# Block attention and a squared-ReLU FFN in one kernel: FFN blocks of four pairs, and one list schedule for all engines

## The chip, the core and the metric

The kernel runs on one core of a Trainium2 chip. The metric is the device time of one execution in microseconds (us); lower is better. The engines are named as the profile names them: PE (TensorE, matmuls; PEld is its weight load), DVE (VectorE), ACT (ScalarE), POOL (GpSimd), SP (SyncE, which issues the DMAs).

## What is computed

```python
def reference(q, k, v, moe_w_in, moe_w_out):        # q, k, v: (8, 8, 576, 64) f32
    # attention inside chunks of 64 positions, each head apart
    scores = q_c @ k_c.T / sqrt(64);  scores -= scores.max(-1)
    attn = exp(scores);  attn /= attn.sum(-1) + 1e-9
    x = (attn @ v_c) -> (4608 tokens, 512)          # heads side by side
    # FFN
    h = x @ w_in                                    # 512 -> 2048, weights in f64
    return (maximum(h, 0) ** 2 @ w_out).astype(f32) # 2048 -> 512
```

## The kernel before

A **pair** is two chunks of 64 positions, 128 tokens of all 8 heads. There are 36 pairs. The FFN runs over **blocks** of pairs, and `blocks` (line 63) is `[4] + [3] * 10 + [2]`: one block of four pairs, ten of three, one of two. For each block and each of the 16 slices `f` of the hidden dimension there is a `Step` (line 608). `mm_in` (L623) makes the hidden slice `h`, 12 matmuls whose moving operand is as wide as the block (128 columns a pair: 512, 384 or 256). ACT and DVE then make `g` from it: `relu`, `square`, `high` (the part `gh` that PE's reduced format holds) and `low` (the rest, `gl`). `mm_out` (L667) adds `g @ w_out` into one PSUM bank a pair, `o`: three matmuls of 512 columns a pair, so 12, 9 or 6 a step. The outs of slice `f` stand two slices behind its ins (`LAG`).

Attention comes in two kinds. The first eight pairs (`NN`) are done whole, as `Pair` (line 487), during the start and block 0. The other 28 pairs are done as 56 **units** of four heads each, in a stacked form: `qst` and `kst` hold high and low parts of q and k in the two halves of the partitions, so that one 256-column matmul a head gives a product at full precision. A unit has on PE four score matmuls `sc` (L353), two transposes `pt` of the probabilities (L403) and four value matmuls `xt` (L437). Between them ACT, DVE and POOL empty the banks, make the softmax, and put `x` into `xh` and `xl`, which are the FFN's input of the *next* block. Two DMAs a unit (`pst<-pst`, L419) copy the high part of the probabilities to the other half of the partitions; the stack of a pair (lines 297 to 318) does the same with four DMAs, `qst<-ql` (L310) and `kst<-kst` (L314).

What sets the order: block 0 with all weight conversion is ordered by a small list scheduler inside the kernel (`Plan`, line 711, used by `first_block`). From block 1 on, only PE's order is written out: `merge` spreads the attention pieces evenly, one matmul at a time, between the FFN matmuls, and the order of the other engines is left to the outer scheduler, with the FFN's ACT and DVE work at a raised priority (`PRIO`). The PSUM banks of attention are two, `at0` and `at1`, taken in turn.

Of the kernel before, what the change touches and what calls it, by code (L numbers as in the profile page):

```python
# [10 lines left out]
F32 = mybir.dt.float32  # L11
# [9 lines left out]
def kernel(  # L21
# [40 lines left out]
    PRIO = 300  # L62
    blocks = [4] + [3] * 10 + [2]
    LAG = 2
    HEAD = 1
    REST = 0
# [10 lines left out]
    NN = sum(blocks[:2]) + 1  # L77
# [13 lines left out]

    early = ctx.enter_context(ExitStack())
    wst = early.enter_context(tc.tile_pool(name="wst", bufs=1))
# [16 lines left out]
    def open_late():  # L110

        early.close()
        pool = ctx.enter_context(tc.tile_pool(name="late", bufs=2))
        late["pool"] = pool
        late["q"] = pool.tile([P, H, 2, CH], F32R, name="qst", tag="qst", bufs=1)
        late["p"] = pool.tile([P, 2, HP, 2, 2, CH], F32R, name="pst", tag="pst", bufs=1)
        load_v(NN)
        nc.gpsimd.memset(late["p"].bitcast(F32), 0.0)
        late["k"] = pool.tile([P, 2, 2, H, CH], F32R, name="kst", tag="kst", bufs=1)
        for c in range(2):  # L120
            r = slice((1 - c) * CH, (2 - c) * CH)
            nc.gpsimd.memset(late["k"].bitcast(F32)[r, 1, c], 0.0)
# [120 lines left out]
    def load_qk(pair):  # L243


        pairs[pair] = {}
        for nm, src in (("q", q), ("k", k)):
            t = raw.tile([P, H, IH, 32], F32, name=f"{nm}_raw{pair}", tag=f"{nm}_raw")
            pairs[pair][nm] = t
            for c in range(2):  # L250
                bb, n0 = divmod(2 * pair + c, NCH)
                for dh in range(DH):
                    r0 = c * D + dh * 32
                    for ih in range(IH):
                        i0 = n0 * CH + ih * 32
                        s = src[bb, :, i0:i0 + 32, dh * 32:(dh + 1) * 32]
                        nc.sync.dma_start(out=t[r0:r0 + 32, :, ih, :], in_=s.rearrange("h i d -> i h d"))

    def load_v(pair):


        if pair < NN:
            for c in range(2):
                bb, n0 = divmod(2 * pair + c, NCH)
                for h2, r in enumerate(halves):
                    s = v[bb, h2:H:2, n0 * CH:(n0 + 1) * CH, :]
                    nc.sync.dma_start(
                        out=vbd[slot_of(pair)][r, :, c, h2, :], in_=s.rearrange("h i d -> i h d")
                    )
            return  # L270
        pairs[pair]["v"] = []
        for c in range(2):
            t = late["pool"].tile([P, H, D], F32, name=f"v_raw{pair}_{c}", tag="v_raw")
            pairs[pair]["v"].append(t)
            bb, n0 = divmod(2 * pair + c, NCH)
            s = v[bb, :, n0 * CH:(n0 + 1) * CH, :].rearrange("h i d -> i h d")
            for r in halves:
                nc.sync.dma_start(out=t[r], in_=s)

    def transpose_pair(pair):  # L280

        for nm in "qk":
            t = late["pool"].tile([P, H, CH], F32, name=f"{nm}t{pair}", tag=f"{nm}t", bufs=1)
            nc.vector.transpose(
                t.rearrange("p h i -> p (h i)"), pairs[pair][nm].rearrange("p h a d -> p (h a d)")
            )
            pairs[pair][nm] = t
        if pair + 1 < NPAIR:
            load_qk(pair + 1)

    def s1(u):
        b, pair, j, hq = units[u]
        if hq == 0:
            yield lambda: transpose_pair(pair)
            yield lambda: stack_qk(pair)

    def stack_qk(pair):

        qt, kt = pairs[pair]["q"], pairs[pair]["k"]
        kst = late["k"]
        qst = late["q"]
        low = late["pool"].tile([P, H, CH], F32R, name=f"ql{pair}", tag="kk", bufs=1)
        for c, (own, oth) in enumerate(other):
            nc.scalar.copy(qst[own, :, c], qt[own])  # L306
        for c, (own, oth) in enumerate(other):
            nc.vector.tensor_tensor(low[own], qt[own], qst.bitcast(F32)[own, :, c], op=ALU.subtract)
        for c, (own, oth) in enumerate(other):
            nc.sync.dma_start(out=qst.bitcast(F32)[oth, :, c], in_=low.bitcast(F32)[own])  # L310
        for c, (own, oth) in enumerate(other):
            nc.scalar.copy(kst[own, 0, c], kt[own])
        for c, (own, oth) in enumerate(other):
            nc.sync.dma_start(out=kst.bitcast(F32)[oth, 0, c], in_=kst.bitcast(F32)[own, 0, c])  # L314
        for c, (own, oth) in enumerate(other):
            nc.vector.tensor_tensor(
                kst[own, 1, c], kt[own], kst.bitcast(F32)[own, 0, c], op=ALU.subtract
            )

    def split_v(u):  # L320
        yield lambda: stack_v(u)

    def stack_v(u):


        b, pair, j, hq = units[u]
        vs = late["pool"].tile([P, 2, HP, 2, D], F32R, name=f"vs{u}", tag="vs")
        ust[u]["v"] = vs
        for c, t in enumerate(pairs[pair]["v"]):
            vr = t[:, hq * HQ:(hq + 1) * HQ].rearrange("p (a b) d -> p a b d", b=2)  # L330
            nc.scalar.copy(vs[:, c], vr)  # L331
            for h2, r in enumerate(halves):
                dst = (r, slice(None), 1 - h2)
                nc.gpsimd.tensor_tensor(  # L334
                    vs[:, c][dst], vr[dst], vs.bitcast(F32)[:, c][dst], op=ALU.subtract
                )
        if hq == NQ - 1 and pair + 1 < NPAIR:
            load_v(pair + 1)

    def s2(u):  # L340


        st = ust[u]
        b, pair, j, hq = units[u]

        def mm2(h):
            if h % 2 == 0:
                st.setdefault("sc", []).append(
                    bank(("at", next(turn_at) % 2), [P, 2, 2, 2, CH], f"sc{u}_{h}")
                )  # L350
            ps = st["sc"][-1][:, h % 2]
            hh = hq * HQ + h
            nc.tensor.matmul(  # L353
                ps.rearrange("p w c j -> p (w c j)"), late["q"][:, hh].rearrange("p c i -> p (c i)"), late["k"][:, :, :, hh],
                start=True, stop=True,
            )

        def half(h):
            if h == 0:
                st["e"] = late["pool"].tile([P, HQ, CH], F32, name=f"e{u}", tag="e", bufs=2)  # L360
            ps, e = st["sc"][h // 2], st["e"][:, h:h + 2]
            for c, r in enumerate(halves):
                nc.scalar.copy(e[r], ps[r, :, 1, c])  # L363
            for c, r in enumerate(halves):
                nc.vector.tensor_tensor(e[r], ps[r, :, 0, c], e[r], op=ALU.add)  # L365

        def rest():
            e = st["e"]
            m = att.tile([P, HQ, 1], F32, name=f"m{u}", tag="m", bufs=2)
            z = att.tile([P, HQ, 1], F32, name=f"z{u}", tag="z", bufs=2)  # L370
            nc.vector.tensor_reduce(m, e, axis=AX.X, op=ALU.max)
            nc.vector.tensor_tensor(e, e, m.broadcast_to([P, HQ, CH]), op=ALU.subtract)
            nc.scalar.activation(e, e, AF.Exp, scale=QSCALE)
            st["e"] = (e, z)

        for h in range(HQ):
            yield lambda h=h: mm2(h)
            if h % 2:
                yield lambda h=h: half(h - 1)
        yield rest  # L380

    def norm(u):
        st = ust[u]

        def f():
            e, z = st["e"]
            nc.vector.tensor_reduce(z, e, axis=AX.X, op=ALU.add)
            nc.vector.tensor_scalar_add(z, z, 1e-9)
            nc.vector.reciprocal(z, z)  # L389
            nc.gpsimd.tensor_tensor(e, e, z.broadcast_to([P, HQ, CH]), op=ALU.mult)  # L390
            st["p"] = e

        yield f

    def s3(u):

        st = ust[u]

        def tr(hp):
            if hp == 0:  # L400
                st["pt"] = bank(("at", next(turn_at) % 2), [P, HP, 2, CH], f"pt{u}")
            ps = st["pt"]
            nc.tensor.transpose(  # L403
                ps[:, hp].rearrange("p a b -> p (a b)"),
                st["p"][:, 2 * hp:2 * hp + 2].rearrange("p a b -> p (a b)"),
                ident,
            )

        for hp in range(HP):
            yield lambda hp=hp: tr(hp)  # L410
# [16 lines left out]
    def s4(u):  # L427
# [14 lines left out]
        def evac(hp):  # L442
# [9 lines left out]
            if hp < HP - 1:  # L452
                return
# [537 lines left out]
```

## Time and profile before

| | before |
|---|---|
| median of three runs | 939.26 us (938.6 to 940.2) |
| span of the profiled execution | 936.9 us |
| PE busy | 920.5 us (98%) |
| DVE busy | 698.3 us (75%) |
| ACT busy | 592.5 us (63%) |
| POOL busy | 212.1 us (23%) |

The profile is of one execution. Times inside it are in us from the start of its span; the median stands 2.4 us above that span. Busy PE means that some matmul was in flight: matmuls overlap, and the row's duration of one matmul (0.39 us for 512 columns) is longer than the distance to the next one's start (0.23 us). So it is the distances of starts, or the length of a run of matmuls in the chain that ended last, that tell what PE can do.

### The profile page before, as it was taken

Reading aid. Unit: us, or ns where it says so; the run is one execution under the profiler, and the core shown is the slowest. Engines: PE = TensorE matmul, PEld = TensorE weight load, DVE = VectorE, ACT = ScalarE, POOL = GpSimd, SP = SyncE. Lnnn points to the kernel's source line nnn. Section 1 sums busy time; section 2 is a strip of 40 time slices with the busy share of each in tenths; the row PEclk is TensorE's granted clock in tenths of the full one; section 3 lists DMA queues with packets and bytes.
Section 4 is the critical chain, followed back from the end, with each engine's and each line's share of the span. In section 5 each row is a group of like instructions: output and inputs, shape, how many; then the busy total and the mean of one; then the engine's idle time right before and its main releaser. Section 6 shows DMA issues by size and latency. Waiting matters only on the chain.

```text
span 936.9 us, 16741 instructions
## 1 busy us (share of the span) xinstructions
PE 920.5 (98%) x5018; PEld 825.2 (88%) x5018; DVE 698.3 (75%) x1607; ACT 592.5 (63%) x1463; POOL 212.1 (23%) x351
## 2 busy tenths in 40 slices
PE   8899999999999999999999999999999999999998
PEld 8788878888899999999999999999989999998997
DVE  5989995788778877877877877877787877753332
ACT  5788875576666666766766766766666666653332
POOL 2000002043222233333322222333333222221000
PEclk9999999999999999999999999999999999999999
DMA  9875505444444543543433543444543442210000
GB/s 197 249 189 175 190 14 121 80 84 103 95 79 76 113 76 76 111 77 74 106 70 71 112 76 67 109 76 79 113 80 75 88 104 57 57 40 12 1 34 23
DMA packets 287193, 85.01 MB, mean 91 GB/s; under 512 B 268672, under 2 KB 276864, under 8 KB 287104
## 3 DMA queue, kind: packets, MB, share of 16 engines
q1 hardware_dynamic: 284992, 83.42, 40.8%
q8 instruction: 41, 0.67, 0.3%
q10 hardware_dynamic: 2112, 0.52, 0.3%
q14 instruction: 48, 0.39, 0.1%
HBM read 52.43 MB, written 9.44 MB: 66 GB/s over the span
## 4 chain that ended last, share of the span: by engine, by line
PE 89%; DVE 6%; DMA 2%; ACT 1%; issue 1%; DVEq 0%; ACTq 0%; SPq 0%
PE h L623 40%; PE o L667 39%; PE sc L353 3%; PE xt L437 3%; PE pt L403 1%; PE sc L527 1%; PE xt L581 1%; DMA kst<-kst 1%; DMA qk_raw<-in_k_dram 0%; DVE gl L650 0%; DVE wia L177 0%; PE k L503 0%; DVE woa L177 0%; ACT qst L306 0%; DVE nz L548 0%
## 5 line engine op out<-in xcount | busy, mean ns | idle before, releaser
L623 PE MATMUL h<-xh,wi 128*128 128x384 f32 (+2 forms) x1536 | 433.7, 339 | 1.8 <-DVE wi L198 1.5
L667 PE MATMUL o<-wo,gh 128*128 128x512 f32 x1152 | 371.7, 396 | 0.0
L623 PEld LDWEIGHTS h<-xh,wi 128*128 128x128 f32 x1536 | 275.0, 188 | 16.0 <-DVE wi L198 1.9
L623 PE MATMUL h<-xl,wi 128*128 128x384 f32 (+2 forms) x768 | 260.5, 339 | 1.2 <-DVE xl L594 1.2
L667 PEld LDWEIGHTS o<-wo,gh 128*128 128x128 f32 x1152 | 208.2, 188 | 33.0
L667 PE MATMUL o<-wo,gl 128*128 128x512 f32 x576 | 226.5, 393 | 0.0
L334 POOL TENSOR_TENSOR vs<-v_raw,vs 64x128 fp32r<-64x128 f32 x224 | 115.8, 517 | 241.4 <-ACT vs L331 227.5
L650 DVE TENSOR_TENSOR gl<-g,gh 128x384 fp32r<-128x384 f32 (+2 forms) x192 | 111.0, 578 | 64.3 <-ACT gh L647 60.5
L623 PEld LDWEIGHTS h<-xl,wi 128*128 128x128 f32 x768 | 144.7, 188 | 8.2 <-DVE xl L594 1.6
L638 DVE TENSOR_TENSOR g<-g 128x384 f32<-128x384 f32 (+1 forms) x176 | 98.5, 560 | 67.5 <-ACT g L634 66.0
L647 ACT CAST gh<-g 128x384 fp32r<-128x384 f32 (+2 forms) x192 | 98.5, 513 | 76.7 <-PE o L667 52.2
L634 ACT ACTIVATE g<-h 128x384 f32<-128x384 f32 (+2 forms) x192 | 94.5, 492 | 79.2 <-PE h L623 57.9
L667 PEld LDWEIGHTS o<-wo,gl 128*128 128x128 f32 x576 | 108.2, 188 | 20.7
L390 POOL TENSOR_TENSOR e<-e,z 128x256 f32<-128x256 f32 x56 | 45.3, 810 | 229.4 <-DVE z L389 66.7
L365 DVE TENSOR_TENSOR e<-sc,e 64x128 f32<-64x128 f32 x224 | 64.7, 289 | 34.4 <-ACT e L363 29.7
L363 ACT COPY e<-sc 64x128 f32<-64x128 f32 x224 | 58.2, 260 | 42.5 <-PE sc L353 39.2
L451 DVE TENSOR_TENSOR x<-xt,x 64x128 f32<-64x128 f32 x224 | 64.6, 289 | 22.3 <-ACT x L449 17.9
L449 ACT COPY x<-xt 64x128 f32<-64x128 f32 x224 | 58.1, 259 | 35.1 <-PE xt L437 31.7
L353 PE MATMUL sc<-kst,qst 128*128 128x256 f32 x224 | 62.9, 281 | 2.0 <-DVE pst L421 1.1
L437 PE MATMUL xt<-pst,vs 128*128 128x256 f32 x224 | 62.7, 280 | 1.8 <-DMA pst<-pst 1.3
L457 POOL TENSOR_TENSOR xl<-x,xh 128x256 fp32r<-128x256 f32 x56 | 44.2, 790 | 59.7 <-ACT xh L456 57.5
L421 DVE TENSOR_TENSOR pst<-pt,pst 64x256 fp32r<-64x256 f32 x112 | 47.3, 422 | 11.0 <-ACT pst L417 7.0
(80 smaller groups left out, 898.1 us busy)
## 6 DMA issues: line engine op xcount, KB each, us to landing
v_raw<-in_v_dram SPq DMA_DIRECT2D x112, 128.0 KB, 3.3
out_dram<-ob SPq DMA_DIRECT2D x36, 256.0 KB, 2.1
wiraw<-in_moe_w_in_dram SPq DMA_DIRECT2D x16, 512.0 KB, 6.1
woraw<-in_moe_w_out_dram SPq DMA_DIRECT2D x16, 512.0 KB, 6.0
q_raw<-in_q_dram SPq DMA_DIRECT2D x224, 32.0 KB, 2.1
k_raw<-in_k_dram SPq DMA_DIRECT2D x224, 32.0 KB, 2.1
qst<-ql SPq DMA_DIRECT2D x56, 128.0 KB, 2.6
kst<-kst SPq DMA_DIRECT2D x56, 128.0 KB, 2.6
```

The source lines that it names most:

```text
L334: nc.gpsimd.tensor_tensor(vs[:, c][dst], vr[dst], vs.bitcast(F32)[:, c][dst], op=ALU.subtract)
L353: nc.tensor.matmul(ps.rearrange("p w c j -> p (w c j)"), late["q"][:, hh].rearrange("p c i -> p (c i)"), late["k"][:, :, :, hh], start=Tru ...
L363: nc.scalar.copy(e[r], ps[r, :, 1, c])
L365: nc.vector.tensor_tensor(e[r], ps[r, :, 0, c], e[r], op=ALU.add)
L437: nc.tensor.matmul(st["xt"][hp][:, c].rearrange("p w a q -> p (w a q)"), st["v"][:, c, hp].rearrange("p a d -> p (a d)"), late["p"][:, :, ...
L451: nc.vector.tensor_tensor(x[r, hp], ps[hp][r, :, 0, h2], x[r, hp], op=ALU.add)
L623: nc.tensor.matmul(self.h[:, :self.n], a[:, c], bb[:, c, :self.n], start=c == 0 and i == 0, stop=c == NCC - 1 and i == 2,)
L634: nc.scalar.activation(self.g, self.h[:, :self.n], AF.Relu)
L638: nc.vector.tensor_tensor(self.g, self.g, self.g, op=ALU.mult)
L647: nc.scalar.copy(self.gh[:, :self.n], self.g)
L650: nc.vector.tensor_tensor(self.gl[:, :self.n], self.g, self.gh.bitcast(F32)[:, :self.n], op=ALU.subtract)
L667: nc.tensor.matmul(acc[b, j], a[:, j * P:(j + 1) * P], bb, start=f == 0 and i == 0, stop=f == NF - 1 and i == 2,)
```

## The change

All nine blocks have four pairs, so that every FFN matmul has 512 columns. `first_block` becomes `program`: the list scheduler now orders all five engines for the whole program, and `merge`, `attention_slot` and the raised priority are gone. In that schedule a unit's four score matmuls are one item, as are its two transposes and its four value matmuls (a **clump** each). They take both attention banks (`scores`, `values`) or one (`turn_p`), are held back to a place in the FFN's order by `PATTERN` and `PERIOD` (3.6 slices a pair; block 2's units are not held back), and start 0.5 us later in the plan than their inputs (`SLACK`). FFN groups of three matmuls have the lowest rank.

Of the stack of q and k, the DMAs are gone: DVE writes q's low part straight into the other half (`q_low`), and ACT copies k's high part there a second time (`k_again`). V is loaded a unit at a time into one buffer (four DMAs a unit, half the size) in place of four a pair. The square is on ACT in blocks 0 and 1 and on DVE after. The two DMAs of the probabilities a unit stay.

```diff
-    blocks = [4] + [3] * 10 + [2]
+    blocks = [4] * 9
-    NN = sum(blocks[:2]) + 1
+    NN = sum(blocks[:2])
...
+        def q_low(self, c):
+            own, oth = other[c]
+            nc.vector.tensor_tensor(
+                late["q"][oth, :, c], self.t["q"][own], late["q"].bitcast(F32)[own, :, c], op=ALU.subtract
+            )
+        def k_again(self, c):
+            own, oth = other[c]
+            nc.scalar.copy(late["k"][oth, 0, c], self.t["k"][own])
...
-        low = late["pool"].tile([P, H, CH], F32R, name=f"ql{pair}", tag="kk", bufs=1)
-            nc.sync.dma_start(out=qst.bitcast(F32)[oth, :, c], in_=low.bitcast(F32)[own])
-            nc.sync.dma_start(out=kst.bitcast(F32)[oth, 0, c], in_=kst.bitcast(F32)[own, 0, c])
...
+    GROUP = 0.69
+    SLACK = 0.5
+    PERIOD = 3.6
+    PATTERN = (("scores", 0, -1.2), ("scores", 1, -0.5), ("turn", 0, 0.5), ("values", 0, 1.4), ("turn", 1, 1.7),
+               ("values", 1, 2.6))
...
+            add(PE, 0.49, x.scores, stacks, both, slack=SLACK, gate=gate)
...
+            add(PE, 0.23, lambda: x.turn_p(which), e + ["ident"], [which], slack=SLACK, gate=gate)
...
+            add(PE, 0.49, x.values,
+                [("vs", i, 0), ("vs", i, 1)] + [(n, h2) for n in ("pst", "pst2", "pst3") for h2 in range(2)],
+                both, slack=SLACK, gate=gate)
...
-    with tc.manual_schedule(engines={PE}):
-        for b in range(1, len(blocks)):
-                merge(ops[n1 * s // ns:n1 * (s + 1) // ns], x)
+    with tc.manual_schedule(engines={PE, DVE, ACT, SP, POOL}):
+        program()
```

What that does to PE's order in the middle of the program, where every block repeats the one ahead. Before, a unit's score matmuls stand one by one between outs (`o`) and ins (`h`):

```order
L667 MATMUL o_0_4547<-wo_1128,gh_8_4912 128x512
L353 MATMUL sc_0_5028<-kst,qst 128x256
L667 MATMUL o_0_4547<-wo_1128,gh_8_4912 128x512
L667 MATMUL o_0_4547<-wo_1128,gl_8_4913 128x512
L667 MATMUL o_1_4552<-wo_1128,gh_8_4912 128x512
L353 MATMUL sc_0_5028<-kst,qst 128x256
L667 MATMUL o_1_4552<-wo_1128,gh_8_4912 128x512
L667 MATMUL o_1_4552<-wo_1128,gl_8_4913 128x512
L667 MATMUL o_2_4561<-wo_1128,gh_8_4912 128x512 x2
L667 MATMUL o_2_4561<-wo_1128,gl_8_4913 128x512
L353 MATMUL sc_2_5051<-kst,qst 128x256
L623 MATMUL h_11_5053<-xh_3517,wi_1237 128x384
```

Now, in block 3, all four stand together, every FFN matmul beside them has 512 columns, and the next clump follows 12 FFN matmuls later:

```order
L625 MATMUL o_1_4169<-wo_499,gh_0_4063 128x512 x2
L625 MATMUL o_1_4169<-wo_499,gl_0_4064 128x512
L347 MATMUL sc_0_4179<-kst,qst 128x256 x2
L347 MATMUL sc_1_4180<-kst,qst 128x256 x2
L625 MATMUL o_2_4187<-wo_499,gh_0_4063 128x512 x2
L625 MATMUL o_2_4187<-wo_499,gl_0_4064 128x512
L625 MATMUL o_3_4196<-wo_499,gh_0_4063 128x512 x2
L625 MATMUL o_3_4196<-wo_499,gl_0_4064 128x512
L588 MATMUL h_3_4205<-xh_3003,wi_582 128x512
```

Ten single insertions a unit have become three clumps. The second place is the end of block 1, where PE now stands like this (`h_0_2814` is the first matmul of block 2, whose input `xh_1885` the last unit completes):

```order
L625 MATMUL o_1_1776<-wo_1492,gl_13_2632 128x512
L386 MATMUL pt_2744<-ident,e_2608 128x128 x2
L625 MATMUL o_2_1785<-wo_1492,gh_13_2631 128x512 x2
L625 MATMUL o_2_1785<-wo_1492,gl_13_2632 128x512
L625 MATMUL o_3_1796<-wo_1492,gh_13_2631 128x512 x2
L625 MATMUL o_3_1796<-wo_1492,gl_13_2632 128x512
L411 MATMUL xt_0_2776<-pst,vs_2574 128x256 x2
L411 MATMUL xt_1_2777<-pst,vs_2574 128x256 x2
L347 MATMUL sc_0_2802<-kst,qst 128x256 x2
L347 MATMUL sc_1_2803<-kst,qst 128x256 x2
L588 MATMUL h_0_2814<-xh_1885,wi_377 128x512
```

Here only six FFN matmuls stand between the last unit's transposes and its value matmuls, and none between those and the block that needs their result. The third place is SP's queue, before in the middle of the program:

```order
L419 DMA pst<-pst 64x4x64 x2
L310 DMA qst<-ql_4994 64x8x64
L314 DMA kst<-kst 64x512
L310 DMA qst<-ql_4994 64x8x64
L314 DMA kst<-kst 64x512
L257 DMA q_raw_5282<-in_q_dram 32x8x32 x3
L278 DMA v_raw_0_5128<-in_v_dram 64x8x64 x2
L278 DMA v_raw_1_5131<-in_v_dram 64x8x64 x2
L419 DMA pst<-pst 64x4x64 x2
```

and now:

```order
L398 DMA pst<-pst 64x4x64 x2
L281 DMA v_raw_5001<-in_v_dram 64x4x64 x2
L250 DMA k_raw_5008<-in_k_dram 32x8x32 x4
L281 DMA v_raw_5001<-in_v_dram 64x4x64 x2
L250 DMA k_raw_5008<-in_k_dram 32x8x32 x4
L281 DMA v_raw_5097<-in_v_dram 64x4x64 x4
L398 DMA pst<-pst 64x4x64 x2
```

The four stack copies of a pair are gone from it, the v loads have doubled in number and stand between the q and k loads, and the copies of the probabilities stand behind them.

## Rows read from the trace of the kernel before

**Rows 1.** The page: busy us, share of the span and instructions of each engine.

```profile
PE 920.5 (98%) x5018; PEld 825.2 (88%) x5018; DVE 698.3 (75%) x1607; ACT 592.5 (63%) x1463; POOL 212.1 (23%) x351
```

**Rows 2.** PE's waits from 147 us on: engine line, releaser, total, times, longest.

```profile
PE pt L403 <- DVE x L451: 1.8, 2, 1.3
...
PE xt L437 <- ACT g L634: 0.5, 1, 0.5
```

**Rows 3.** Chain that ended last: start, length, line, count of matmuls.

```profile
56.39 2.72 PE h L623 x12
...
136.18 4.52 PE h L623 x22
140.70 2.72 PE o L667 x12
...
151.38 2.10 PE h L623 x12
153.48 2.08 PE o L667 x9
...
891.06 1.43 PE h L623 x12
892.50 1.39 PE o L667 x6
```

**Rows 4.** PE in order of time: start, length, instruction; four outs' starts.

```profile
140.54 0.62 PE L667 MATMUL o<-wo,gh 128*128 128x512 f32 x2
...
142.58 0.62 PE L667 MATMUL o<-wo,gh 128*128 128x512 f32 x2
...
148.45 0.63 PE L667 MATMUL o<-wo,gh 128*128 128x512 f32 x2
...
150.53 0.61 PE L667 MATMUL o<-wo,gh 128*128 128x512 f32 x2
```

**Rows 5.** One steady block: stretch, its length, busy PE PEld DVE ACT POOL, granted clock.

```profile
401.95:475.70 73.75, 73.75 (x398) 66.99 (x397) 58.25 (x141) 48.98 (x131) 21.83 (x37) 1.00 0.43 86
```

**Rows 6.** The chain in block 0: outs behind a clump of scores, and four transposes.

```profile
70.12 2.14 PE o L667 x9
...
77.03 0.44 PE pt L566 x4
```

**Rows 7.** A steady unit in order of time, from its last transpose to its first value matmul.

```profile
502.99 0.27 PE L403 MATMUL pt<-ident,e 128*128 128x128 f32 x1
...
503.77 1.29 SPq L419 DMA_DIRECT2D pst<-pst  x2
...
508.61 0.28 PE L437 MATMUL xt<-pst,vs 128*128 128x256 f32 x1
```

**Rows 8.** The same of a late unit, where PE waits (in brackets).

```profile
845.25 0.27 PE L403 MATMUL pt<-ident,e 128*128 128x128 f32 x1
...
849.04 0.36 PE L437 MATMUL xt<-pst,vs 128*128 128x256 f32 x1 [1.32 <-DMA pst<-pst]
```

**Rows 9.** Groups by line and shape: busy us, mean ns of one, idle before.

```profile
L451 DVE TENSOR_TENSOR x<-xt,x 64x128 f32<-64x128 f32 x224 | 64.6, 289 | 22.3 <-ACT x L449 17.9 <-PE o L667 0.2
...
L449 ACT COPY x<-xt 64x128 f32<-64x128 f32 x224 | 58.1, 259 | 35.1 <-PE xt L437 31.7
...
L457 POOL TENSOR_TENSOR xl<-x,xh 128x256 fp32r<-128x256 f32 x56 | 44.2, 790 | 59.7 <-ACT xh L456 57.5
...
L312 ACT CAST kst<-kt 64x512 fp32r<-64x512 f32 x56 | 34.7, 620 | 1.3
...
L456 ACT CAST xh<-x 128x256 fp32r<-128x256 f32 x56 | 22.7, 405 | 43.5 <-DVE x L451 43.4
...
L594 DVE TENSOR_TENSOR xl<-xt,xh 128x512 fp32r<-128x512 f32 x8 | 5.5, 684 | 3.4 <-ACT xh L592 3.4
```

**Rows 10.** DMA issues: KB each, median us from issue to landing.

```profile
pst<-pst SPq DMA_DIRECT2D x112, 64.0 KB, 2.2
```

**Rows 11.** Busy time and granted clock (the third number from the end) near the start.

```profile
28.30:31.60 3.30, 3.30 (x18) 2.86 (x17) 2.60 (x6) 2.04 (x4) 0.00 (x0) 0.50 1.05 372
```

More of the change, by code (lines that the diff above doesn't have):

```diff
@@ L320, in split_v @@
[L320 to L380, printed above, removed]
@@ L723, in __init__, with add @@
             self.readers = {}
+            self.last = {}
             self.rank = 0
[L726 removed]
+        def add(self, engine, cost, fn, reads=(), writes=(), size=0, line=None, slack=0.0, gate=None):
             n = len(self.ops)
@@ L744, in run @@
             ops = self.ops
-            end = {}
-            free = {}
+            need = [len(before | after) for _, _, _, before, after, _, _, _ in ops]
+            then = [[] for _ in ops]
+            for n, (_, _, _, before, after, _, _, _) in enumerate(ops):
+                for x in before | after:
+                    then[x].append(n)
+            ready = {e: [] for e in (PE, DVE, ACT, SP, POOL)}
+            free = dict.fromkeys(ready, 0.0)
+            end = [0.0] * len(ops)
             queue = 0.0
-            left = list(range(len(ops)))
@@ L774, in run @@
                 order.append((t, n))
-                left.remove(n)
+                for x in then[n]:
+                    need[x] -= 1
+                    if not need[x]:
+                        admit(x)
             for _, n in sorted(order):
@@ L874, in square @@
[L874 to L886 removed]
+                k = (s.b * NF + s.f) * 2 * NCC + c
@@ new lines, in program @@
+        for n in range(NF):
+            slice_of(n)
+        p.rank = 1000
+        add(POOL, 0.1, open_late, [], ["early", "late"])
+        for c in range(2):
+            add(POOL, 1.0, lambda c=c: zero_late(c), ["late"], [("kst3", c), ("pst3", c)])
+        first = NQ * NN
+        values_in(first)
+        order = []
+        for pair in range(NN, NPAIR):
+            b = block_of[pair]
+            at = NF * (b - 1) + PERIOD * (pair - first_pair[b])
+            u = NQ * pair
+            for what, i, off in PATTERN:
+                order.append((at + off, u + i, what))
@@ new lines, in program @@
+        n = NF
+        for when, u, what in sorted(order):
+            if units[u][0] == 2:
+                when = NF
+            while n <= when:
+                slice_of(n)
+                n += 1
+            p.rank = 1000 + 2 * u
+            gate = groups[min(int(when * 2 * NCC), max(groups))] if when > NF else None
+            if what == "scores":
+                if u == first:
+                    stack(units[u][1])
+                scores(u, gate)
+                split(u)
+                if units[u][3] == NQ - 1 and units[u][1] + 1 < NPAIR:
+                    p.rank += 1
+                    stack(units[u][1] + 1)
+            elif what == "turn":
+                probabilities(u, gate)
+            else:
+                values(u, gate)
```

581 lines of the change are left out of this document (319 added, 262 removed).

## The prediction

> **What bounds the kernel now.** I read the page first: PE is busy for 98% of the span [rows 1]. A busy PE need not be a full one, so the next view is who PE waits for. From 147 us on, where block 0's FFN ends, PE waits 5.4 us in 789 (five rows, from 1.8 to 0.5 us) [rows 2]. In the steady middle a block of three pairs takes 73.75 us with PE busy for all of it, DVE for 58.25 and ACT for 48.98 [rows 5]. So the time is the number of matmuls by the distance of their starts, and the third view, the chain in order of time, gives that distance. The reader should read lengths of runs there, not durations of single matmuls.
>
> Twelve outs of 512 columns among others of 512 take 2.72 us, 0.2267 each (at 140.70 us) [rows 3], and twelve ins of 512 the same (at 56.39 us) [rows 3]. In a three-pair block without attention the ins of 384 columns take 2.10 and the nine outs 2.08 us, a step of 4.18 (at 151.38 us) [rows 3]. Nine outs should take 9 × 0.2267 = 2.04. Set side by side, they do where they follow 512-column ins (140.54 to 142.58), and take 2.08 where they follow 384-column ins (148.45 to 150.53) [rows 4]. So PE loses about 0.04 us after each change of width, spread over the next nine matmuls. A second cost shows by width: 512, 384 and 256 columns at 2.4 GHz are 213.3, 160 and 106.7 ns; what the rows give is 226.7, 2.10 / 12 = 175 and 1.43 / 12 = 119 [rows 3]. About 13 ns stand on top of each matmul whatever its width. Fewer, wider matmuls and fewer changes of width are thus worth something although no column is saved.
>
> **The change part by part.**
>
> *FFN width.* A step takes 2.72 + 2.72 = 5.44 us for four pairs, 4.18 for three, 1.43 + 1.39 = 2.82 for two [rows 3]. Before: 16 × (5.44 + 10 × 4.18 + 2.82) = 801.0 us. After: 16 × 9 × 5.44 = 783.4. That is **−17.6 us**, all of it on PE's own row, which is the bound. 576 matmuls fewer by 13 ns make 7.5 of it; the changes of width the rest. The lower bound is that the matmuls never settle: at the unsettled 2.08 / 9 = 0.231 us, 3456 of them take 798.7, and the gain is 2.3.
>
> The Trainium skill, page "TensorE: Matmul & The Clock Gate", section "Wait — 56ns, not 53.3ns?", speaks against this: it puts the fixed cost at about 2.5 ns a matmul, whatever its width. By it 576 fewer would bring only 1.4 us of the 7.5, and the sum below would come out 6.1 us later. The trace does not agree: 13 ns at all three widths [rows 3].
>
> *Attention in clumps.* Before, a steady block holds six units: 73.75 − 16 × 4.18 = 6.87, or 1.14 us a unit [rows 3, 5]. That is little more than the eight 256-column matmuls (8 × 0.119 = 0.95) and two transposes (0.44 / 4 = 0.11 each [rows 6]), 1.17 together, because single insertions fall into stretches that a change of width has unsettled already. After, the stretches around are settled, and each of three clumps pays its 0.04: 0.95 + 0.22 + 0.12 = 1.29. For 56 units that is **+8.4 us**. Bounds: 0 (a clump costs what single insertions cost now) and +18.5: nine outs behind a clump of 16 small matmuls took 2.14 in place of 2.04 [rows 6], and 0.10 in place of 0.04 for 168 clumps is 10.1 more. I take 1.29, since that clump was four times as long.
>
> *PE's waits.* The schedule holds a clump back until its inputs are due, and gives FFN groups in the meantime, so that I read from the order where PE has nothing left to give. That is the end of block 1. Between the last unit's transposes and its values stand six outs, 6 × 0.227 = 1.4 us; where PE waited in the trace, transpose to values took 849.04 − 845.25 = 3.8 [rows 8]. So 2.4 of wait there. Then block 2 needs that unit's x: four copies at 0.259, an add of 0.289, the cast 0.405, POOL's 0.790 [rows 9], 2.5 us, against 0.5 us of score matmuls and one matmul of 0.23: 1.8 more. 4.2 us in all, and up to 1.7 more if the clock falls to 1.2 GHz for a stretch as long as the one near the start (3.3 us at 0.50 granted) [rows 11]. Before, the same stage holds most of the 5.4 us of waits, as units of block 2 are made in haste there too; I take those away. In the steady part I allow 1.5 us, see the rivals. Block 0's order on PE is the same up to its last slices; ahead of its last weights DVE now has pair 7's `xl`, 0.68 us [rows 9], and PE waits for those weights: +0.7. Waits together: 4.2 + 1.5 + 0.7 − 5.4 = **+1.0 us**; bounds −4 and +10.
>
> *Work moved off PE.* `k_again` adds two casts of 0.620 a pair on ACT [rows 9], 35 us in all; DVE writes q's low part into the other half in the same number of instructions. Taken by block, as an estimate from 4/3 of a three-pair block [rows 5]: ACT 65.3 + 5.0 for `k_again`, some 70 us in 97.4, and DVE 77.7, less a little for wider instructions; 72% and 80%. Nothing on the path, as long as each chain has its room. If a shifted write took twice as long, DVE would have 1.4 us a pair more, still beside PE. The stack's four DMAs a pair leave SP and four v loads come: 28 issues a pair before and after. What is queued behind a v load that waits for its single buffer is the copy of the probabilities; that is the rival below. Evictions: four a block in place of three on the same four banks, hidden by the 2.72 us of the next block's ins; if not, at most one store's landing (about 2 us) a block.
>
> Sum: −17.6 + 8.4 + 1.0 = −8.2 us against the span of 936.9, so 928.7. The median stands 2.4 above that span, and I add it: **931 us**, 0.9% faster.
>
> **The rivals.**
>
> *A. The chain from transposes to values is longer than its room (slower).* Now five of eight units of a steady block have 24 FFN matmuls between them (5.5 us), two have 21 (4.8) and one has 30, by the order. For: the chain goes through ACT, an SP issue and a DMA of 2.2 us [rows 10], and in the order the copies stand behind v and q loads in SP's queue, where they stood alone or behind q loads before. Against: the chain took 3.8 us where PE waited for it [rows 8], and a steady unit's 5.6 us were without wait [rows 7], with its two copies issued by 505.1, so landed near 507.3, 4.3 us after the transpose. The price over six blocks with chain length C is 6 × (2 × (C − 4.8) + 5 × (C − 5.5)). The gain of 8 us is gone at C = 5.5; at 6.0 it is 29 us, and the time 959. Chance 0.12 for 942 or more.
>
> *B. FFN matmuls do not settle between clumps (about the same).* After each clump nine matmuls are slow, and a steady block has 16 between two clumps on average, so some gaps are too short. If all run at 0.231, the width brings 2.3 us in place of 17.6, and clumps cost no more than insertions do now: 936.9 − 2.3 + 1.0 = 935.6, median 938. Against: block 0's ins run at 0.227 some 4 us behind a clump of 16 small matmuls (at 56.39 us) [rows 3]. Chance 0.13. The fixed cost that the Trainium skill gives on that page would end near the same place, 931 + 6.1 = 937; as the rows stand against it, I give it 0.01 of this chance.
>
> *C. Clumps cost nothing more (faster still).* If the 0.04 us is a matter of the FFN's own width changing at every half step, it is not paid among 512s of one width: 931 − 8.4 = 922.6. For: every slow series in my rows stands where 384 turns to 512 [rows 4]. Against: the nine outs of block 0, among 512s alone, were slow behind a clump [rows 6]. Chance 0.12.
>
> **How the numbers follow.** The forecast, 925 to 937, has 0.63; A 0.12, B 0.13, C 0.12. The range of 8 in 10 leaves out A and the far end of C: 920 to 940. A measurement of this kernel tells 0.2% from no change, 1.9 us, so faster is below 937.4 and slower above 941.1. Faster: 0.63 + 0.12 + a third of B, 0.79. Same: the rest of B, 0.08. Slower: A and a little for block 1's end taking over 10 us, 0.13.
>
> **What would show it.** Right: in the profile after, the steady block of four pairs takes 16 × 5.44 + 8 × 1.29 = 97.4 us; twelve ins or outs without a clump between take 2.72; PE waits nowhere in the middle, and some 4 us near 240 to 250 us, at the first matmul of block 2 and the values ahead of it. B shows as runs of twelve at 2.77, C as a block of 96.2 us. A shows as waits of `xt` for DMA `pst`, in each block at the same two places. The prediction would be wrong as a whole if ACT or DVE, 10% fuller than now in block 1 where the square is on ACT too, held back `gh` or `gl`, with waits of the outs.

## The result, and the profile after

The changed kernel takes **930.71 us** (median of four runs, 929.78 to 931.86) against 939.62 for the kernel before on the same chip (938.6 to 940.2): a ratio of 0.9903, 95% interval 0.9889 to 0.9917. The forecast was 931, with a range of 920 to 940. The profiled execution has a span of 928.0 us, against 936.9. First comes the line of the changed kernel's page that answers to [rows 1]: PE has 576 matmuls fewer, and ACT is fuller.

```profile
span 928.0 us, 15256 instructions
...
PE 911.7 (98%) x4442; PEld 760.5 (82%) x4442; DVE 694.8 (75%) x1500; ACT 620.7 (67%) x1434; POOL 217.1 (23%) x352
```

Next, a steady block of four pairs, which answers to [rows 5] (stretch, its length, busy PE, PEld, DVE, ACT, POOL, granted clock, DMA share, GB/s). The forecast was 97.4 us, with 78 for DVE and 70 for ACT. This is the shortest of the four alike blocks (3 to 6), which take 97.3 to 97.7 us from first in-matmul to first in-matmul:

```profile
441.63:538.91 97.28, 97.28 (x465) 81.22 (x464) 79.67 (x179) 68.43 (x171) 30.77 (x48) 1.00 0.33 66
```

Here are lines of the chain that ended last, in the block ahead of that one (start, length, line, matmuls). Twelve matmuls take 2.72 where no clump stands before them, and nine behind a clump 2.07 in place of 2.04. A clump of scores takes 0.47 in most places and 0.67 here: by the starts in the trace, two short gaps (0.12 and 0.07 us) stand ahead of its third and fourth matmul:

```profile
350.08 2.72 PE h L588 x12
...
353.96 2.07 PE o L625 x9
...
371.62 2.72 PE o L625 x12
...
381.88 0.67 PE sc L347 x4
```

PE's waits from 147 us on answer to [rows 2] (in total, times, longest). Two are left above 0.15 us, both at the end of block 1:

```profile
PE xt L411 <- DMA pst<-pst: 2.4, 1, 2.4
PE sc L347 <- DVE x L425: 1.2, 1, 1.2
```

The same place in the chain shows six outs (five of them from 238.28), the landing of the copied probabilities, the values, the scores behind the x of the last unit, and then nine ins that take 3.29 us, where nine behind a clump take 2.07 elsewhere:

```profile
238.28 1.16 PE o L625 x5
...
239.77 2.16 DMA pst<-pst
...
242.07 0.49 PE xt L411 x2
...
244.00 0.49 PE sc L347 x2
...
245.38 3.29 PE h L588 x9
```

In two stretches the granted clock (third number from the end) fell, once behind the wait for the last weights of block 0 and once behind the waits just shown. A mean of 0.66 over 5 us, and of 0.86 over 10, is 3.4 and 2.8 us at 1.2 GHz in place of 2.4:

```profile
124.00:129.00 5.00, 4.32 (x12) 3.41 (x13) 4.83 (x11) 3.24 (x7) 0.00 (x0) 0.66 0.00 0
245.00:255.00 10.00, 10.00 (x43) 8.21 (x43) 7.31 (x19) 7.46 (x19) 2.46 (x5) 0.86 0.27 54
```

Last, the end of the program. The last two of the last block's four results wait for a store to leave their buffer; one such store, of 2.03 us, is on the chain:

```profile
921.57 0.70 DVE ob L634
...
922.28 2.03 DMA out_dram<-ob
...
924.43 0.69 DVE ob L634
```

### The profile page after: what moved, and what is told of

Same layout as the page of the kernel before. It is cut to its first block, busy times and chain, and to the rows that moved or that the text cites. A ratio compares the mean times of both kernels' runs of the same rounds, so it can differ in the third digit from the quotient of the medians.

```text
span 928.0 us, 15256 instructions
## 1 busy us (share of the span) xinstructions
PE 911.7 (98%) x4442; PEld 760.5 (82%) x4442; DVE 694.8 (75%) x1500; ACT 620.7 (67%) x1434; POOL 217.1 (23%) x352
## 4 chain that ended last, share of the span: by engine, by line
PE 93%; DVE 4%; DMA 1%; issue 1%; ACT 1%; DVEq 0%; ACTq 0%
PE h L588 42%; PE o L625 41%; PE sc L347 3%; PE xt L411 3%; PE pt L386 1%; PE sc L499 1%; DMA pst<-pst 1%; PE xt L553 1%; DMA qk_raw<-in_k_dram 0%; DVE wia L174 0%; DVE nz L520 0%; DVE wia L181 0%; DVE xl L566 0%; PE k L475 0%; DVE wi L195 0%
## 5 line engine op out<-in xcount | busy, mean ns | idle before, releaser
L588 PE MATMUL h<-xh,wi 128*128 128x512 f32 x1152 | 397.8, 396 | 2.1 <-DVE wi L195 1.7
L588 PEld LDWEIGHTS h<-xh,wi 128*128 128x128 f32 x1152 | 217.9, 189 | 46.3 <-DVE wi L195 2.1
L588 PE MATMUL h<-xl,wi 128*128 128x512 f32 x576 | 226.2, 393 | 1.6 <-DVE xl L566 1.6
L599 ACT ACTIVATE g<-h 128x512 f32<-128x512 f32 x144 | 86.2, 599 | 98.8 <-PE h L588 92.7
L615 DVE TENSOR_TENSOR gl<-g,gh 128x512 fp32r<-128x512 f32 x144 | 105.4, 732 | 56.5 <-ACT gh L612 54.9
L612 ACT CAST gh<-g 128x512 fp32r<-128x512 f32 x144 | 89.4, 621 | 61.0 <-PE o L625 56.4
L603 DVE TENSOR_TENSOR g<-g 128x512 f32<-128x512 f32 x112 | 87.3, 780 | 53.7 <-ACT g L599 51.8
L588 PEld LDWEIGHTS h<-xl,wi 128*128 128x128 f32 x576 | 109.3, 190 | 21.3 <-DVE xl L566 1.9
L403 DVE TENSOR_TENSOR pst<-pt,pst 64x256 fp32r<-64x256 f32 x112 | 47.3, 422 | 21.6 <-ACT pst L393 20.0
L393 ACT CAST pst<-pt 64x256 fp32r<-64x256 f32 x112 | 41.2, 368 | 20.7 <-PE pt L386 18.1
L335 ACT CAST vs<-v_raw 128x256 fp32r<-128x256 f32 x112 | 43.0, 405 | 12.0 <-DMA v_raw<-in_v_dram 9.4
```

What stands on the lines that cost most here:

```text
L403: nc.vector.tensor_tensor(pst[own, 1, :, :, h2], self.pt[own], pst.bitcast(F32)[own, 0, :, :, h2], op=ALU.subtract)
L588: nc.tensor.matmul(self.h[:, :self.n], a[:, c], bb[:, c, :self.n], start=c == 0 and i == 0, stop=c == NCC - 1 and i == 2,)
L599: nc.scalar.activation(self.g, self.h[:, :self.n], AF.Relu)
L603: nc.vector.tensor_tensor(self.g, self.g, self.g, op=ALU.mult)
L612: nc.scalar.copy(self.gh[:, :self.n], self.g)
L615: nc.vector.tensor_tensor(self.gl[:, :self.n], self.g, self.gh.bitcast(F32)[:, :self.n], op=ALU.subtract)
```

## Experiments

**The FFN alone, in both kernels.** The forecast rests on 17.6 us from the width of the blocks. With the attention of the later pairs left out, the two FFNs should differ by about that.

```diff
-        for pair in range(NN, NPAIR):
+        for pair in range(0):          # the changed kernel; in the one before: slots = [[]]
...
-            xh, xl = xt[self.b]
+            xh, xl = xt[self.b % 2]
```

> The kernel before without the attention of all pairs from the eighth on; the FFN of the third block and later reads the x of the first two blocks. What is left is the FFN of blocks of 4, ten of 3, and 2. Theory (the FFN's width is worth 17.6 us and 56 units of attention cost 1.14 to 1.19 us each before): a block of three pairs takes 16 x 4.18 = 66.9 us in place of 73.75, PE waits nowhere after block 0, and the span falls from 936.9 by 64 to 67 us of units and 5.3 of waits to about 866. Rival (attention is hidden in gaps that the FFN has anyway): the block stays above 70 us and the span above 890.

> The changed kernel without the same attention, nine blocks of 4. Theory: a block takes 16 x 5.44 = 87.0 us, and the span falls from 928.0 by 56 x 1.29 = 72 us of units and some 5 us of waits and clock at the end of block 1 to about 850, so 16 us (14 to 18) below the FFN alone before. Rival B (matmuls of 512 columns do not settle, 0.231 us each): a block of 88.7 us, span 865, about the same as the FFN alone before. Rival C (clumps cost no more than the insertions before): the same 850 would be the changed kernel less 64, so 859.

Measured, in one run each: 872.28 us (span 870.5) and 870.82 us (span 869.0). For the kernel before, that is 4.5 us above what was expected (a block takes 16 × (2.11 + 2.09) = 67.2 us); for the changed kernel it is 19 above. These lines are from the chain of the FFN alone, first before, then after:

```profile
304.29 2.11 PE h L623 x12
306.41 2.09 PE o L667 x9
```

```profile
301.83 2.80 PE o L625 x12
304.63 2.80 PE h L588 x12
```

Matmuls of one width, with nothing at all between them, take 2.80 us a dozen (0.2331 each) for hundreds of us, where the changed kernel takes 2.72. A change of width cannot be the reason, since there is none. The number is near the 2.77 that rival B names for matmuls that never settle, but no clump is there to keep them from it. Two things differ from the changed kernel: the other engines are emptier, and small tiles of the attention are missing, so that x, g, gh and gl lie 128 bytes lower in SBUF (the on-chip memory that holds the operands).

**Addresses.** A matmul reads two operands from SBUF, a stationary one (its weights) and a moving one. In the built programs of both kernels, weights, x, gh and gl all begin 160 bytes behind a multiple of 256, so that each FFN matmul's two operands are a multiple of 256 bytes apart. In the two runs above, x, gh and gl begin 32 bytes behind one, the weights still 160. In the next run each block reads and writes them at a shift of its own.

```diff
+    pad = att.tile([P, 32], F32, name="pad")
+    SHIFT = [0, 0, 0, 32, 64, 128, 192, 256, 384]
...
-            xh, xl = xt[self.b % 2]
+            s = SHIFT[self.b] // 4
+            xh, xl = (x[:, s:s + NCC * 4 * P].rearrange(...) for x in xs[self.b % 2])
...
-                gp.tile([P, MAXB * P], F32R, name=f"g{m}{s}", tag=f"g{m}", bufs=GBUFS) for m in "hl"
+                gp.tile([P, MAXB * P + MORE], F32R, name=f"g{m}{s}", tag=f"g{m}", bufs=GBUFS)[
+                    :, SHIFT[self.b] // 4:SHIFT[self.b] // 4 + MAXB * P] for m in "hl"
```

> The FFN alone in nine blocks of 4, as in the run of the changed kernel without attention, where twelve matmuls took 2.80 us and not 2.72. There the x and g tiles lay 128 bytes lower than in the changed kernel, since small tiles of the attention were missing. Here they lie as in the changed kernel, and blocks 3 to 8 read x and write gh and gl further on by 32, 64, 128, 192, 256 and 384 bytes (x is then shifted data; blocks 0 to 2 by 0). Theory (the place of the operands in SBUF sets the pace): blocks 1 and 2 run at 2.72 a dozen, 87.0 us a block, the block at 128 at 2.80, 89.5 us, the others at one or the other or something new. Rival (the pace needs the clumps, or the work of the other engines): 2.80 in every block, span 869.

Measured: 862.37 us (one run, span 860.6). The blocks shifted by 0, 32, 64, 128, 192 and 256 bytes, in this order:

```profile
229.21:316.25 87.04, 87.04 (x386) 72.10 (x384) 23.52 (x34) 20.75 (x35) 0.00 (x0) 1.00 0.04 13
316.25:405.77 89.52, 89.52 (x386) 72.06 (x385) 23.56 (x34) 20.70 (x35) 0.00 (x0) 1.00 0.03 12
405.77:494.97 89.20, 89.20 (x385) 72.14 (x384) 23.53 (x34) 20.67 (x35) 0.00 (x0) 1.00 0.03 12
494.97:584.07 89.10, 89.10 (x385) 72.20 (x384) 23.55 (x34) 20.67 (x35) 0.00 (x0) 1.00 0.03 12
584.07:673.35 89.28, 89.28 (x386) 72.13 (x384) 23.53 (x34) 20.65 (x35) 0.00 (x0) 1.00 0.03 12
673.35:760.44 87.09, 87.09 (x385) 72.08 (x384) 23.52 (x34) 20.72 (x35) 0.00 (x0) 1.00 0.04 13
```

Shifts of 0 and 256 give 87.04 and 87.09 us a block, 16 × 5.44. The others give 89.1 to 89.5, with 2.78 to 2.80 a dozen; the last block (384) has 2.80 too. The other engines do the same work in all of them, and the granted clock is 1.00. So the pace of the FFN has two values, and the place of the operands chooses between them. The expectation that the place sets the pace is borne out; its rival, that the pace needs the clumps or the work of the other engines, is not.

**The changed kernel at the slow place, and the kernel before there.** Two small tiles of the attention move from the pool ahead of x to one behind it. Nothing else changes; every engine has the same instructions in the same order.

```diff
-            self.m = att.tile([P, HQ, 1], F32, name=f"m{self.u}", tag="m", bufs=2)
+            self.m = raw.tile([P, HQ, 1], F32, name=f"m{self.u}", tag="m", bufs=2)
...                                                     # z in the same way
```

> The changed kernel in its own order, with x, g, gh and gl 128 bytes lower in SBUF (two small tiles of the attention lie behind them in place of ahead). Theory of the place: FFN matmuls never come below 0.2331 us; 3456 of them by 6.4 ns are 22 us, of which those right behind clumps pay a part already: median 943 to 951. Rival (the pace needs the clumps): 931, no change.

> The kernel before in its own order, with x, g, gh and gl 128 bytes lower in SBUF, as in the run of the changed kernel that lost its gain by that. Theory (operands that are not a multiple of 256 bytes apart keep matmuls at the slow pace): the outs of the kernel before are slow already (0.231 to 0.232 us, behind narrower ins), so only block 0's 768 matmuls (some 4 us, as far as they are not slow behind clumps) and 1920 ins of 384 columns lose, 1.5 ns each as in the two runs without attention (176.0 against 174 to 174.5 ns), 3 us: median 941 to 946, and both kernels moved stand within 0.5% of each other. Rival (every matmul of 512 columns loses 6 ns wherever it stands): 1919 of them, 12 us, 950.

Measured: the changed kernel moved takes 940.84 us, 1.0022 of the kernel before (95% interval 1.0010 to 1.0033). That is below the 943 to 951 expected, and its whole gain is gone. The kernel before moved takes 942.62, 1.0042 of the kernel before unmoved (1.0025 to 1.0060), within what was expected. At the slow place the change is thus worth 0.2% in place of 1%, and the two intervals hardly tell that from nothing. In the changed kernel moved, a dozen takes 2.80 also in the last block, where no clump stands:

```profile
861.02 2.80 PE h L588 x12
863.81 2.80 PE o L625 x12
```

Here are a steady block of it, and one of the kernel before moved (unmoved it takes 73.75 [rows 5]):

```profile
445.05:543.68 98.63, 98.63 (x465) 81.09 (x464) 78.96 (x179) 68.11 (x171) 30.32 (x48) 1.00 0.33 65
```

```profile
369.61:443.67 74.06, 74.06 (x399) 67.31 (x397) 58.26 (x142) 48.96 (x131) 21.87 (x37) 1.00 0.43 86
```

Of 98.63 us the FFN alone has 89.5 at this place, so that eight units cost 9.1, 1.14 each; at the fast place it is (97.28 − 87.04) / 8 = 1.28. The slow place thus has the same 1.14 as the kernel before. This fits the reading that a unit's extra 0.14 us is what it costs to fall out of the fast pace; where there is no fast pace, its clumps cost their own matmuls. Hence the changed kernel moved lost 1.2%, 11 us, by the two ratios, where nine blocks of its FFN alone lose 22 (89.5 against 87.04); the units make 56 × 0.14 = 8 us of what lies between. The kernel before loses only 0.31 us a block: its outs run at 0.231 anyway, and a step goes from 2.10 + 2.08 [rows 3] to the 2.11 + 2.09 above.

**The place itself, or the distance.** In the scan the weights stayed, so that place and distance moved together. Here all FFN operands move together, to multiples of 256. The slack of the clumps is 0, as in the run without slack below, with which it is to be compared.

```diff
-    SLACK = 0.5
+    SLACK = 0.0
+    pad = const.tile([P, 24], F32, name="pad")      # ahead of the weights; the pool att goes behind g, its m and z share a tile
```

> No slack, and weights, x, g, gh and gl all begin on a multiple of 256 bytes, where they begin 160 behind one in the changed kernel (distances between them stay multiples of 256). Theory (only the distance between the two operands counts): blocks of 97.3 us as in the run without slack, 2.72 a dozen, span 926. Rival (the place itself counts): a dozen below 2.72, down to 2.56 if the 13 ns a matmul were a matter of place, or slower than 2.72.

Measured: 930.63 us (one run, span 928.8; the run without slack has 926.1). A dozen takes 2.72, here in the last block, and a steady block 97.47:

```profile
880.29 2.72 PE h L590 x12
883.01 2.72 PE o L627 x12
```

```profile
344.77:442.24 97.47, 97.47 (x465) 80.95 (x464) 78.87 (x179) 67.93 (x171) 29.73 (x48) 1.00 0.33 66
```

So the pace goes with the distance, as far as these places tell: x on a multiple of 256 with the weights left at 160 was not run. Beginning on a multiple of 256 brings nothing by itself, and the 13 ns a matmul stay. The block is 0.2 us longer than without slack alone (97.27), and PE waits 0.8 us more in block 1; why is open.

**Blocks of three in the new schedule.** This run is to part the width from the schedule.

```diff
-    blocks = [4] * 9
+    blocks = [4] + [3] * 10 + [2]
...
-    PERIOD = 3.6
+    PERIOD = 4.8
```

> The new list schedule and its clumps, but the blocks of the kernel before (4, ten of 3, 2), a pair of units every 4.8 slices in place of 3.6. Theory (the width is the whole gain, the schedule brings nothing by itself): the FFN takes 17.6 us more than in the changed kernel; clumps cost between 1.14 us a unit (as single insertions did, where changes of width have unsettled the stretch) and 1.29: median 940 to 948. Rival (the new order of all engines is the gain, and width little): 930 to 934.

Measured: 978.77 us, a ratio of 1.0418 (1.0380 to 1.0456), far above both expectations. PE's largest waits:

```profile
PE pt L386 <- DVE x L425: 13.5, 22, 1.8
PE xt L411 <- DMA pst<-pst: 11.4, 11, 5.4
```

The second line is rival A of the prediction, in another kernel than the one that was forecast: values wait for the copied probabilities. In the first line, transposes wait for the bank of the values before them. The offsets of the clumps are counted in slices, a slice shrank from 5.44 to 4.18 us, and the room of each chain with it. The schedule's model also took a group of in-matmuls of 384 columns for as long as one of 512. Both were changed in one run:

```diff
-    PATTERN = (("scores", 0, -1.2), ("scores", 1, -0.5), ("turn", 0, 0.5), ("values", 0, 1.4), ("turn", 1, 1.7),
-               ("values", 1, 2.6))
+    PATTERN = (("scores", 0, -1.6), ("scores", 1, -0.67), ("turn", 0, 0.67), ("values", 0, 1.87), ("turn", 1, 2.27),
+               ("values", 1, 3.47))
...
-                groups[k] = add(PE, GROUP, ...
+                groups[k] = add(PE, (0, 0, 0.36, 0.53, GROUP)[blocks[s.b]], ...
```

> Blocks of 4, ten of 3, 2 in the new list schedule again, with the offsets of the clumps stretched by 4/3 (slices of 4.18 us in place of 5.44) and the model's cost of the narrower in-matmuls made 0.53 and 0.36 in place of 0.69 a group. Theory (36 us of waits in the first try came from the room, and the width is the gain): under 12 us of waits in all, span 937 to 947. Rival (clumps do not go with blocks of three at all): waits stay near 36 us, span above 960.

Measured: 953.43 us (one run, span 951.6, which is 4.6 above the expected range). PE's waits are 16.7 us in place of 36, 6.0 of them at the end of block 1, and behind these the clock is at 0.75 over 10 us. Which of the two edits took the waits away is open. A steady block, which answers to [rows 5]:

```profile
374.64:449.61 74.97, 74.78 (x399) 67.38 (x397) 59.12 (x142) 52.05 (x136) 21.84 (x37) 1.00 0.32 64
```

It takes 74.97 us against 73.75 with single insertions: in blocks of three, clumps cost 0.2 us a unit more, and the schedule by itself gains nothing. With this run the change can be parted, roughly. The first column is the end of PE's last matmul less all waits above 60 ns, from the starts in the trace; the third is what is left from there to the end of the span:

| | PE without waits | waits of PE | behind the last matmul | span |
|---|---|---|---|---|
| before | 921.9 | 11.3 | 3.6 | 936.9 |
| three_fitted | 930.6 | 16.7 | 4.3 | 951.6 |
| changed kernel | 913.1 | 9.8 | 5.1 | 928.0 |

From the first line to the second, schedule and clumps, it is +8.6 us; from the second to the third, width, −17.5. Two things besides stand in these differences. One is the clock. Before, PE worked at 1.2 GHz for one stretch near 30 us [rows 11], and in the changed kernel for the two stretches shown above, of 3.4 us each; three_fitted has two:

```profile
29.00:32.40 3.40, 3.40 (x18) 2.81 (x18) 3.20 (x6) 1.91 (x4) 0.00 (x0) 0.50 1.05 374
216.70:226.90 10.20, 5.59 (x19) 5.24 (x20) 3.71 (x12) 3.71 (x12) 3.11 (x7) 0.50 0.38 68
```

Half of PE's busy time in them is an estimate of what they cost: 1.7 us before, 4.5 in three_fitted, 3.4 in the changed kernel. The other is the eighth pair. `NN` is the number of pairs in the first two blocks, 7 in three_fitted, where the other two kernels have 8; so one pair more goes as two units (2.7 us at the 1.35 of its steady block) and not whole. A whole pair has on PE two sets of four transposes for q and k, and the scores, transposes and values, 4.8 us by the chain of the kernel before (0.44 for each set of transposes, [rows 6]):

```profile
97.08 1.73 PE xt L581 x16
98.81 0.44 PE q L503 x4
...
104.55 1.73 PE sc L527 x16
```

With both taken out, again as an estimate, schedule and clumps are about +8 us and width about −18.5.

**A fixed cost for each matmul.** Here the columns stay, and the in-matmuls double in number; each has its own weight load.

```diff
-            nc.tensor.matmul(self.h[:, :self.n], a[:, c], bb[:, c, :self.n], ...)
+            for n, r in enumerate((slice(0, 2 * P), slice(2 * P, 4 * P))):
+                nc.tensor.matmul(self.h[:, r], a[:, c], bb[:, c, r], ...)
```

> Each in-matmul of 512 columns is made in two of 256; columns and everything else stay. 1728 more matmuls. Theory (13 ns on each matmul at every width, 0.04 us lost in the nine outs behind a change of width): the ins of a step take 24 x 0.119 = 2.86 in place of 2.72, 144 steps make +20 us, the 144 changes of width up to +6; span 948 to 954. Rival (2.5 ns a matmul): +4 us, or +10 with the changes of width; span 932 to 938.

Measured: 947.71 us (one run, span 945.9, so +17.9), 2 below the expected range and far from the rival. The chain shows nine outs and then 24 ins of 256 columns:

```profile
346.68 2.07 PE o L626 x9
348.75 2.87 PE h L589 x24
```

2.87 in place of 2.72 makes 0.15 × 144 = 21.6 us, of which 17.9 arrive. By the starts in the trace a steady block takes 99.53 us in place of 97.28, so 2.25 more, which would be 18 in eight blocks; block 0, where PE waits for weights, is no longer than it was. That is 13 ns for each of 24 matmuls in place of 12, as the prediction has it. A change of width costs 0.03 us in the last block, where twelve outs behind such ins take 2.75 and not 2.72 (from 853.95 us, for one); the +6 for it does not show in the total. Every matmul here, as in all these kernels, has its own weight load (6170 of each), so whether the 13 ns belong to the matmul or to the load is open. The Trainium skill ("TensorE: Matmul & The Clock Gate", section "Wait — 56ns, not 53.3ns?") puts the fixed cost at about 2.5 ns, by which the run would have been some 4 us longer, as an estimate (1728 × 2.5 ns). This trace does not agree.

**No slack.** A clump is issued as soon as the schedule's model allows, not 0.5 us later.

```diff
-    SLACK = 0.5
+    SLACK = 0.0
```

> The changed kernel with the slack of a clump 0 in place of 0.5: the schedule gives a clump as soon as its own model says that its inputs are there. By the order the room from transposes to values is 21 or 24 matmuls (4.8 or 5.4 us) in a steady block, and no clump is left at the end of block 1. Theory (the slack costs nothing in the steady part and holds the units of block 1 back): the 3.6 us of waits at the end of block 1 and some 1.4 us of clock go, and the chain of 3.8 us still fits: 925 to 927. Rival A (the chain takes more than its room at times): waits of xt for pst in every block, 931 or more.

Measured: 927.79 us, 0.9883 of the kernel before (0.9858 to 0.9907), 0.8 above the expected 925 to 927. The gain over the changed kernel, 0.2%, lies within the intervals; the trace shows what it comes from. From 246 us on, PE waits for this and no more, and the clock from 235 to 255 us stays at 1.00:

```profile
PE xt L411 <- DMA pst<-pst: 0.4, 1, 0.4
PE pt L386 <- DVE x L425: 0.2, 1, 0.2
```

```profile
235.00:255.00 20.00, 19.34 (x90) 15.46 (x89) 13.08 (x33) 14.73 (x36) 6.14 (x10) 1.00 0.32 60
```

The waits of 3.6 us and the clock behind them are gone. Smaller waits come in block 1, 1.3 us in all, so that PE's waits in the table's count go from 9.8 to 8.2. Rival A does not come: the least room from the end of the transposes to the values is 4.6 us by the starts in the trace, as in the steady blocks of the changed kernel.

**No slack, and four buffers at the end.** The last block's third and fourth results leave by buffers of their own.

```diff
+            if self.b == len(blocks) - 1 and j > 1:
+                o = raw.tile([P, DM], F32, name=f"ob{self.b}_{j}", tag="qk"[j - 2] + "_raw")
```

> No slack, and the last block's four results leave through four buffers (two of them the raw q and k tiles that are free by then) in place of two. After the last matmul of the changed kernel the third and fourth copy wait for a store of 2.0 us. Theory: that wait goes, 1.5 to 2 us less than without slack alone (927.8): 926. Rival (the four stores then share the queue and end no earlier): 927.8.

Measured: **925.71 us**, 0.9859 of the kernel before (0.9839 to 0.9878), the fastest here. By its ratio that is 0.24% or 2 us under no slack alone; the intervals overlap. The chain now ends without a wait for a store:

```profile
917.78 3.41 PE o L625 x15
...
921.21 0.69 DVE ob L638
```

**One piece of the change undone.** k's second copy goes by DMA again, not by ACT.

```diff
-            nc.scalar.copy(late["k"][oth, 0, c], self.t["k"][own])
+            nc.sync.dma_start(out=f[oth, 0, c], in_=f[own, 0, c])       # f = late["k"].bitcast(F32)
```

> The changed kernel with one part undone: the second copy of k's high part in the stack goes by two DMAs a pair on SP's queue, as in the kernel before, and not by two casts of 0.62 us on ACT. Theory (ACT's 35 us of casts lie beside PE, SP's two more issues a pair too): 930 to 932, and no new wait of PE in the steady blocks. Rival (the copies of the probabilities stand behind the new DMAs in SP's queue, and their room of 4.6 to 6.7 us is used up): waits of xt for pst in the steady blocks, 935 or more.

Measured: 931.03 us, 0.9913 (0.9891 to 0.9934), the same as the changed kernel within the intervals. From 250 us on PE waits 0.6 us, not counting waits below 0.15:

```profile
PE xt L412 <- DMA pst<-pst: 0.4, 1, 0.4
PE xt L412 <- ACT e L373: 0.2, 1, 0.2
```

The move of that copy to ACT costs and brings nothing that shows, as counted.

## Why the prediction was right, and where not

- **The bound.** PE, by the distance of starts: right. Every experiment that changed this distance moved the time, and the one that took 35 us of casts from ACT did not.
- **FFN width, −17.6 us.** Measured −17.5 by the table above, about −18.5 with the clock and the eighth pair taken out; that the table comes so close is in part luck. The size was right, but its condition was not seen. The prediction took 2.72 a dozen as what matmuls of one width come to when they settle. It is what they come to when, besides, their operands are a multiple of 256 bytes apart, and it is luck that both kernels have them so. Its lower bound, 2.3 us if they never settle, is about what the whole change is worth at the slow place (0.2%). Of the 17.6, changes of width are not all the rest beside 7.5: they make 160 × 0.04 = 6.4, and the ins of 384 columns 1920 × 2 ns = 3.8, since their row gives 15 ns on top and not 13.
- **13 ns a matmul.** This held for 256 columns in ins_in_halves, and stayed with all operands on multiples of 256 bytes. It is no constant of the matmul: at the slow distance 512 columns take 0.2331 us, 20 ns on top.
- **Clumps, +8.4 us.** The forecast was 1.29 us a unit; the steady blocks give 1.28 to 1.33, and schedule and clumps together come to +8.6 by the table, about +8 as an estimate without the rest. The prediction calls 1.14 a little more than the 1.17 of the bare matmuls, where it is a little less. Its reason, that a stretch that is unsettled already hides an insertion, is supported by the 1.14 at the slow place.
- **Waits, +1.0 us.** At the end of block 1, 2.4 and 1.2 were measured for 2.4 and 1.8, and 1.4 us of clock (0.14 of 10 us), which was named as possible. In the steady part it is 0.15 for 1.5. In block 0 the sum of +0.7 came out at +0.8, but for other reasons: PE began its FFN 1.1 us earlier (36.19 against 37.27), the last weights made it wait 0.3 more, and the clock behind that wait took 1.6 (ten ins in 4.14 us from 124.68, 2.56 before). Less the 5.4 of before that is +0.6 in all. The earlier start goes with the clock and not with the change: over the fourteen profiled executions, of both kernels and their variants, the FFN gets going at 36.2 to 36.6 us in the three whose clock did not fall near 30 us (the changed kernel's is one), at 36.4 to 37.3 in the eight with 3.4 us at 1.2 GHz there, and at 37.4 to 38.0 in the three with 6.9. So that 1.1 is, in the main, luck of one execution.
- **Evictions.** These are hidden between blocks, as counted, but the end of the program was forgotten: four results by two buffers leave PE's last matmul 5.1 us ahead of the end in place of 3.6. That 1.5 us is the one term with no place in the sum.
- **Rivals.** A did not come; what it costs shows in blocks_of_three. C did not come: a block takes 97.3 us and more, not 96.2. B was the near one: its time, 938, is that of moved_128_bytes within 3 us, but its condition, clumps too close together, is not what decides. A few small tiles, 128 bytes of them, would have done. Nothing in the trace of before shows this, since there its operands never leave the good distance.

As measured, PE without waits fell by 8.8 us (about −18.5 for width, +8 for schedule and clumps, +1.7 for the clock), its waits by 1.5 (9.8 against 11.3), and the end grew by 1.5. That is −8.9 with rounding, where −8.2 was forecast, and 928.0 for the span where 928.7 was forecast.

## What to carry to other kernels

Count a matmul-bound stretch by the distance of starts, from long runs in the chain, and ask of each pace under which condition it holds. Here 2.8% of the FFN's time hung on where the pools put the tiles, and an edit that adds or drops a small tile can make or lose more than the edit itself. A variant that leaves work out moves tiles too, so compare addresses before drawing a conclusion from it. In a list schedule that counts room in steps, the room shrinks with the step; and a wait ahead of PE costs more than its length where the clock falls behind it, as at 245 us here.

## What was not expected of the hardware

- In this kernel the distance between a matmul's stationary and moving operand in SBUF sets the pace of 512-column matmuls: 0.2267 us at multiples of 256 bytes (shifts of 0 and 256), 0.232 to 0.233 at shifts of 32, 64, 128, 192 and 384. At 384 columns the slow place has 2.11 a dozen, where the good one has 2.10 at most [rows 3]. Why is open: no view of the profile used here shows it, and other data types were not tried.
- At the good distance the pace is the same whether DVE, ACT and DMA have much work or little: 87.04 us a block with DVE at 27% and no attention (16 × 2 dozens of 2.72), and the same 2.72 a dozen in a block of the full kernel with DVE at 82%.
